# A fused attention and GEGLU kernel: batch 0's causal mask moved to TensorE, one normalisation per head pair, a third gate/value buffer, and batch 2's loads spread over batch 1

## The chip, the cores and the metric

The kernel runs on one core of a Trainium2 chip. The metric is the time of one execution on the device, in microseconds (us). A kernel is run several times, and the median is quoted with the lowest and highest run. The experiments were run in three sets, each on another chip (a1 to a4; b1 to b4; b5, c1, c2 and d1), with the kernel before beside each set: its medians were 399.49, 399.61 and 399.82 us. The ratios refer to these, and a difference between medians of two sets carries some tenths of a us for that.

One execution of each kernel was taken with the hardware profiler. Its span is about 1.7 us shorter than the device time of the same run (398.1 against 399.8 us before). The engines are PE (TensorE), DVE (VectorE), ACT (ScalarE), POOL (GpSimd) and SP (SyncE); PEld is TensorE's weight load. "The array" below is TensorE's.

## The reference

Eight batches of causal attention, with 16 "beacon" keys that every query may see. The result, regrouped as 4608 tokens of 512 numbers, goes through a GEGLU feed-forward.

```python
B, H, S, Nb, D = 8, 8, 576, 16, 64
k_all = concat([beacon_k, k], axis=2);  v_all = concat([beacon_v, v], axis=2)
scores = q @ k_all.T / sqrt(D)
scores = where(causal, -1e9, scores)       # causal only in the columns after the 16 beacons
a = softmax(scores);  attn = a @ v_all
x = attn.transpose(0, 2, 1, 3).reshape(4608, 512)
out = (gelu(x @ w_gate) * (x @ w_val)) @ w_out      # 512 -> 1536 -> 512
```

## The kernel before

The inputs are float32 and are converted as they are loaded; on the chip everything is bf16 with float32 accumulation in PSUM. Heads are handled in pairs, four pairs a batch. While batch b's attention runs, TensorE fills its waits with the output products (`out_mms`) of the chunk of tokens before; then comes batch b's feed-forward stage, the twelve gate/value products. Scores lie transposed (keys on partitions); each pair has four chunks of them, and each chunk gets one exponential on ScalarE and then its masks:

```python
def scores(b, m, c):
    ...
    for t, s_lo, w, col in CHUNKS[c]:
        for hi in range(2):
            r = slice(64 * hi, 64 * hi + 64)
            mm(s_ps[:, hi, col : col + w], qkT[r, m, 1, t * P : (t + 1) * P],
               qkT[r, m, 0, NB + s_lo : NB + s_lo + w], True, True)
    act(expT[:, :, o : o + w], s_ps[:, :, 0:w], ACT.Exp, scale=QK_SCALE)
    if b:
        masks(b, m, c)          # GpSimd: affine_select with 0.0, in place

# batch 0 only: masks(0, m, c, by_dve=True) takes the minimum with a 0 / 3e38 triangle on VectorE
```

The weighted sum of values carries the softmax denominator as a 65th column (`DV = 65`). Ten slots of 65 columns do not fit one bank, so they lie as six in one bank and four in the next, and the normalisation is done per bank:

```python
for c0, j0, n in ((0, 0, 6), (512, 6, 4)):
    x = x_ps[:, c0 : c0 + n * DV].rearrange("p (j d) -> p j d", d=DV)
    reciprocal(r, x[:, :, D:DV])
    tensor_tensor(out=y_sb[:, j0 : j0 + n, :], in0=x[:, :, 0:D], in1=r.to_broadcast([P, n, D]), op=mult)
```

`turn` then transposes `y_sb` on TensorE and `put` copies it to `xT_sb`, the input of the feed-forward. The order within a batch, and where loads are issued:

```python
if b:
    o(6); ab(0); o(8); cd(0); o(6); ab(1); o(4); av(b, 0); cd(1); o(4); turn(b, 0); put(b, 0)
    ...                                   # o(n): n output products; av: weighted sum + normalisation
    o(4); av(b, 3)
    gv_mms(b, 0, 0, 1, 2); turn(b, 3); put(b, 3); gv_mms(b, 1, 0, 1, 2); gv_mms(b, 0, 3); gv_mms(b, 1, 3)
for fi in range(F_TILES):                 # 12 gate/value products
    if fi < 2: gv_close(b, fi)            # GELU on ScalarE, product with the value half on VectorE
    else:      gate_val(b, fi)            # psum_s has two buffers of two banks
    ...
    if fi == 0:
        if b + 2 < B:
            load_qk(b + 2); load_v(b + 2)           # 17 loads, all issued by GpSimd
        if NPERM <= b + 1 < B:
            transpose_dma(b + 1)                    # keys and queries of batches 2 to 7, turned by DMA
```

GpSimd therefore has two jobs in one program order: it issues all the loads, and it masks the exponentials of batches 1 to 7.

The softmax here doesn't subtract the row's maximum and nothing guards it: scores larger than these inputs give would overflow.

## Time and profile before

| | before |
|---|---|
| device time, median of three (lowest to highest) | 399.53 us (399.45 to 400.36); 399.49 with the fourth run used below |
| span of the profiled run | 398.1 us, granted clock 0.987 |
| period of batches 2 to 6 (first output product of one attention stage to that of the next) | 42.60 us |
| period of batch 1 | 46.41 us (50.35 to 96.76) |
| from the first output product of batch 7 to the end | 88.35 us |

The page's first part for the kernel before, busy time, share of the span and number of instructions of each engine:

```profile
PE 377.9 (95%) x3014; PEld 183.4 (46%) x3014; DVE 166.9 (42%) x342; ACT 189.0 (47%) x254; POOL 159.8 (40%) x287
```

TensorE is the limit; a gain must come from the 5% in which it waits. The ends of matmuls in the trace are modelled, so gaps are read from starts: a 512-column matmul starts every 0.216 us, four of them take 0.87 us. The waits view of the kernel before, TensorE alone; the columns are what waits and for what, then us in all, times, and the longest:

```profile
PE gv_ps L161 <- DVE hT_sb L357: 6.9, 7, 1.0
PE x_ps L161 <- POOL expT L259: 1.6, 1, 1.6
```

The first wait comes seven times, once in each feed-forward stage after batch 0. The timeline shows one of them. A timeline line is: start, duration, engine, line, operation, output<-inputs, shape, count, and in brackets the idle time before it and what ended that (hT_sb, the "hidden product" below, is GELU of the gate half times the value half):

```profile
163.34 0.38 PE L161 MATMUL gv_ps<-xT_sb,wv_sb 128*128 128x512 bf16 x1
164.69 1.02 PE L161 MATMUL gv_ps<-xT_sb,wg_sb 128*128 128x512 bf16 x4 [0.98 <-DVE hT_sb L357]
```

The single value product would be followed 0.22 us after its start, at 163.56; the next one starts at 164.69. The time between, 1.13 us here (1.14 before rounding), is the wait for one of two gate/value buffers; 0.98 of it is in the brackets, the rest hidden by the modelled end of the matmul before. Seven such waits of 1.14 are 8.0 us.

Two further losses show little in the waits view. The first is in the turn of each pair; the timeline of TensorE in batch 3 of the kernel before:

```profile
146.37 1.08 PE L161 MATMUL x_ps<-v_sb,expT 128*128 128x65 bf16 x30
...
147.78 1.04 PE L161 MATMUL o_ps<-wo_sb,hT_sb 128*128 128x512 bf16 x4
148.88 0.45 PE L169 MATMUL y_ps<-ident,y_sb 128*128 128x128 bf16 x5
```

The four output products that cover VectorE's normalisation end at 147.78 + 0.87 = 148.65, but the turn starts at 148.88, 0.23 us later. VectorE's own timeline shows why, four chained operations from 147.49 to 148.83:

```profile
147.49 0.20 DVE L307 RECIPROCAL r_sb<-x_ps 128x6 f32<-128x6 f32 x1 [0.22 <-PE x_ps L161]
147.72 0.56 DVE L309 TENSOR_TENSOR y_sb<-x_ps,r_sb 128x384 bf16<-128x384 f32 x1
148.19 0.17 DVE L307 RECIPROCAL r_sb<-x_ps 128x4 f32<-128x4 f32 x1
148.40 0.43 DVE L309 TENSOR_TENSOR y_sb<-x_ps,r_sb 128x256 bf16<-128x256 f32 x1
```

The second is at the beginning of batch 1. Timeline of TensorE, kernel before:

```profile
56.43 1.04 PE L161 MATMUL o_ps<-wo_sb,hT_sb 128*128 128x512 bf16 x4
59.10 1.10 PE L161 MATMUL x_ps<-v_sb,expT 128*128 128x65 bf16 x15 [1.63 <-POOL expT L259]
60.43 1.01 PE L161 MATMUL x_ps<-v_sb,expT 128*128 128x65 bf16 x15 [0.24 <-DMA v_sb<-in_v_dram]
```

After 57.30 (56.43 + 0.87) the array has nothing until the first mask is done and it starts again at 59.10; a further wait of 0.24 us follows, and then 15 small matmuls take 1.01 us, twice the usual pace. The view puts the 0.24 us down to a transfer, but the fifth mask ends at 60.37 and the next matmul starts at 60.43, while batch 1's own values had landed by 49.61; so it is most likely the masks again. GpSimd's timeline of the same stretch shows what its masks waited behind: 6.07 us idle, ended by a transfer of the output weight, and then the issue of the loads themselves:

```profile
45.90 3.31 POOL L112 DMA_DIRECT2D q_sb<-in_q_dram  x4 [6.07 <-DMA wo_sb<-in_moe_w_out_dram]
...
54.37 4.27 POOL L112 DMA_DIRECT2D v_sb<-in_v_dram  x5
58.54 1.83 POOL L259 TENSOR_SCALAR_AFFINE_SELECT expT<-expT 128x224 bf16<-128x224 bf16 x5
```

The windows view of the kernel before, two stretches of 5 us (busy time with counts of PE, PEld, DVE, ACT, POOL; then PEclk, the granted TensorE clock; the recorded time of DMA packets over the time of the 16 DMA engines, which can exceed 1; GB/s):

```profile
10.00:15.00 5.00, 5.00 (x68) 2.92 (x65) 4.56 (x11) 3.66 (x5) 5.00 (x8) 0.50 2.17 162
...
60.00:65.00 5.00, 4.76 (x45) 2.42 (x42) 1.72 (x5) 1.89 (x3) 2.09 (x7) 0.66 0.79 95
```

In batch 0 (first line) ScalarE, VectorE, GpSimd and TensorE are all busy at a low recorded clock; the second line is the slow stretch after the wait in batch 1.

### The profile page before, as it was taken

Reading aid. Unit: us, or ns where it says so; the run is one execution under the profiler, and the core shown is the slowest. Engines: PE = TensorE matmul, PEld = TensorE weight load, DVE = VectorE, ACT = ScalarE, POOL = GpSimd, SP = SyncE. Lnnn points to the kernel's source line nnn. Section 1 sums busy time; section 2 is a strip of 40 time slices with the busy share of each in tenths; the row PEclk is TensorE's granted clock in tenths of the full one; section 3 lists DMA queues with packets and bytes.
Section 4 is the critical chain, followed back from the end, with each engine's and each line's share of the span. In section 5 each row is a group of like instructions: output and inputs, shape, how many; then the busy total and the mean of one; then the engine's idle time right before and its main releaser. Section 6 shows DMA issues by size and latency. Waiting matters only on the chain.

```text
span 398.1 us, 7407 instructions
## 1 busy us (share of the span) xinstructions
PE 377.9 (95%) x3014; PEld 183.4 (46%) x3014; DVE 166.9 (42%) x342; ACT 189.0 (47%) x254; POOL 159.8 (40%) x287
## 2 busy tenths in 40 slices
PE   6999989899999999899989999999989998999995
PEld 3464435444554445444544455444544454444442
DVE  2754634533363434432553344443534344333332
ACT  3763265424753387236733574348623772322210
POOL 8955394860468135841485047613300240000000
PEclk9799998999999999999999999999999999999999
DMA  7999994899139920997199915992141010000112
GB/s 106 178 206 204 177 159 59 96 145 109 54 65 146 143 57 29 134 148 75 55 96 141 92 54 83 140 127 63 45 102 28 30 54 26 2 0 28 43 50 91
DMA packets 140273, 36.24 MB, mean 91 GB/s; under 512 B 126928, under 2 KB 135632, under 8 KB 140240
## 3 DMA queue, kind: packets, MB, share of 16 engines
q0 software_dynamic: 104960, 19.13, 63.7%
q1 hardware_dynamic: 35280, 16.66, 21.5%
q8 instruction: 23, 0.38, 0.4%
q14 instruction: 10, 0.08, 0.1%
HBM read 38.27 MB, written 9.44 MB: 120 GB/s over the span
## 4 chain that ended last, share of the span: by engine, by line
PE 72%; DMA 11%; DVE 10%; POOL 3%; issue 1%; ACT 1%; POOLq 0%
PE gv_ps L161 39%; PE o_ps L161 19%; DVE y_sb L309 7%; PE x_ps L161 7%; DMA wo_sb<-in_moe_w_out_dram 5%; PE s_ps L161 4%; PE y_ps L169 3%; DMA wv_sb<-in_moe_w_val_dram 3%; DMA v_sb<-in_v_dram 3%; DVE r_sb L307 2%; DVE hT_sb L357 1%; POOL qk L112 1%; DMA k_sb<-in_k_dram 1%; ACT ge_sb L164 1%; POOL q_sb L112 1%
## 5 line engine op out<-in xcount | busy, mean ns | idle before, releaser
L164 ACT ACTIVATE ge_sb<-gv_ps 128x512 bf16<-128x512 f32 x108 | 63.6, 597 | 154.2 <-PE gv_ps L161 152.1
L357 DVE TENSOR_TENSOR hT_sb<-gv_ps,ge_sb 128x512 bf16<-128x512 f32 x108 | 74.0, 691 | 123.2 <-ACT ge_sb L164 123.2
L161 PE MATMUL gv_ps<-xT_sb,wg_sb 128*128 128x512 bf16 x432 | 113.8, 379 | 6.9 <-DVE hT_sb L357 6.9
L164 ACT ACTIVATE expT<-s_ps 128x1024 bf16<-128x1024 f32 (+3 forms) x128 | 103.6, 861 | 31.9 <-PE s_ps L161 31.5
L161 PE MATMUL gv_ps<-xT_sb,wv_sb 128*128 128x512 bf16 x432 | 113.8, 379 | 0.0
L161 PE MATMUL o_ps<-wo_sb,hT_sb 128*128 128x512 bf16 x432 | 108.0, 382 | 0.0
L259 POOL TENSOR_SCALAR_AFFINE_SELECT expT<-expT 128x256 bf16<-128x256 bf16 (+2 forms) x145 | 52.8, 388 | 131.8 <-ACT expT L164 131.8
L161 PEld LDWEIGHTS <-wg_sb 128*128 128x128 bf16 x432 | 41.0, 98 | 54.5 <-issue 8.8
L161 PEld LDWEIGHTS <-wv_sb 128*128 128x128 bf16 x432 | 42.2, 98 | 50.9
L161 PEld LDWEIGHTS <-hT_sb 128*128 128x128 bf16 x432 | 37.4, 98 | 49.8 <-issue 11.0
L385 DVE COPY o_sb<-o_ps 128x512 f32<-128x512 f32 x36 | 24.9, 690 | 44.9 <-PE o_ps L161 44.7
L112 POOL DMA_DIRECT2D v_sb<-in_v_dram x40 | 33.6, 855 | 15.0 <-DMA k_sb<-in_k_dram 5.7
L161 PEld LDWEIGHTS <-expT 128*128 128x128 bf16 (+1 forms) x960 | 33.6, 98 | 9.4 <-POOL expT L259 2.7
L161 PE MATMUL s_ps<-qkT 64*128 64x336 bf16 (+5 forms) x384 | 36.2, 290 | 1.2 <-ACT qkT L164 0.7
L161 PE MATMUL x_ps<-v_sb,expT 128*128 128x65 bf16 x930 | 34.3, 194 | 2.0 <-POOL expT L259 1.6
L309 DVE TENSOR_TENSOR y_sb<-x_ps,r_sb 128x384 bf16<-128x384 f32 (+1 forms) x62 | 30.4, 491 | 2.1
L112 POOL DMA_DIRECT2D q_sb<-in_q_dram x30 | 25.2, 859 | 6.1 <-DMA wo_sb<-in_moe_w_out_dram 6.1
L112 POOL DMA_DIRECT2D k_sb<-in_k_dram x30 | 25.5, 878 | 3.3 <-DMA q_sb<-in_q_dram 3.0
L307 DVE RECIPROCAL r_sb<-x_ps 128x6 f32<-128x6 f32 (+1 forms) x62 | 11.4, 184 | 35.7 <-PE x_ps L161 35.7
L161 PEld LDWEIGHTS <-qkT 64*128 64x128 bf16 x384 | 13.0, 96 | 17.2 <-issue 11.1
L328 DVE COPY xT_sb<-y_ps 128x576 bf16<-128x576 bf16 x31 | 14.1, 455 | 13.0 <-PE y_ps L169 13.0
L169 PEld LDWEIGHTS <-y_sb 128*128 128x128 bf16 (+1 forms) x160 | 9.3, 98 | 17.7 <-DVE y_sb L309 16.8
(41 smaller groups left out, 102.5 us busy)
## 6 DMA issues: line engine op xcount, KB each, us to landing
out_dram<-o_sb SPq DMA_DIRECT2D x36, 256.0 KB, 2.0
v_sb<-in_v_dram POOLq DMA_DIRECT2D x24, 128.0 KB, 9.8
q_sb<-in_q_dram POOLq DMA_DIRECT2D x24, 128.0 KB, 6.7
k_sb<-in_k_dram POOLq DMA_DIRECT2D x18, 128.0 KB, 9.8
wo_sb<-in_moe_w_out_dram POOLq DMA_DIRECT2D x1, 1536.0 KB, 18.4
wg_sb<-in_moe_w_gate_dram POOLq DMA_DIRECT2D x2, 512.0 KB, 11.2
wv_sb<-in_moe_w_val_dram POOLq DMA_DIRECT2D x2, 512.0 KB, 12.8
v_sb<-in_v_dram POOLq DMA_DIRECT2D x8, 112.0 KB, 9.0
```

The lines of the kernel that those rows point to most:

```text
L112: keep(nc.gpsimd.dma_start(out=out_ap, in_=in_ap))
L161: keep(nc.tensor.matmul(out_ap, lhsT, rhs, start=start, stop=stop, **kw))
L164: keep(nc.scalar.activation(out_ap, in_ap, func, **kw))
L169: keep(nc.tensor.transpose(out_ap, in_ap, ident[0:n, 0:n]))
L259: nc.gpsimd.affine_select(out=d, in_=d, pattern=[[0, 2], [1, n]], compare_op=ALU.is_ge, fill=0.0, base=NB if t == 0 else 0, channel_multip ...
L307: keep(nc.vector.reciprocal(r, x[:, :, D:DV]))
L309: nc.vector.tensor_tensor(out=y_sb[:, j0 : j0 + n, :], in0=x[:, :, 0:D], in1=r.to_broadcast([P, n, D]), op=ALU.mult)
L328: keep(nc.vector.tensor_copy(out_ap, y_ps[:, 0:S]))
L357: nc.vector.tensor_tensor(out=h_of[ci][:, fi, :], in0=gv_ps[:, 1, :], in1=ge_sb, op=ALU.mult)
L385: keep(nc.vector.tensor_copy(o_sb[:, ti, :], o_ps))
```

## The change

The intent, in five parts:

1. **Third gate/value buffer.** In batches 1 to 7 the third product takes the bank pair of `psum_x`, which is free by then. One gate/value half is moved ahead of the last turn.
2. **One normalisation per pair.** The two heads of a pair now lie in one bank each, five slots of 65 columns, so that one reciprocal and one product cover both banks.
3. **Batch 0's mask in PSUM.** Matmuls add -1e6 above the diagonal to the scores before the exponential; VectorE and GpSimd lose their mask steps there.
4. **Loads.** Batch 2's loads leave GpSimd's queue ahead of batch 1's masks. Its queries and keys are issued in and after batch 1's attention, its values after it. From batch 3 on, loads are issued two batches ahead as before.
5. **Order of batch 0**: transposes in halves, weighted sums in other banks, one pair's transposes of batch 1 moved into batch 1.

Part 3 rests on accumulation into part of a bank: the matmul of the scores starts the group, the mask matmuls that follow do not. The Trainium skill ("PSUM — Partial Sum Buffer", The four PSUM rules) says that a matmul without the first flag adds where a hidden written-bit is set and overwrites where it is not; this case agrees as far as its results go, for every run with these matmuls was correct against the reference.

```diff
 # scores(): batch 0's mask
+            diag = b == 0 and s_lo == S_LO[t]
             for hi in range(2):
                 mm(s_ps[:, hi, col : col + w], ...
-                    True, True,
+                    True, not diag, skip_group_check=True,
+            if diag:
+                base, n = (NB if t == 0 else 0), DIAG[t]
+                for k0, width in ((0, min(n, 64 - base)), (64, n)):
+                    for hi in range(2):
+                        r = slice(64 * hi, 64 * hi + 64)
+                        mm(s_ps[:, hi, col : col + width], eye[r, 64 - k0 : 192 - k0],
+                           neg[r, 64 - k0 + base : 64 - k0 + base + width], False, k0 == 64, ...)
 # normalize()
-        for c0, j0, n in ((0, 0, 6), (512, 6, 4)):
-            x = x_ps[:, c0 : c0 + n * DV].rearrange("p (j d) -> p j d", d=DV)
+        for x_ps, h0, h1 in x_of.pop(i):           # [(x, 0, 2)], a tile of two banks
+            x = x_ps[:, :, 0 : 5 * DV].rearrange("p b (j d) -> p b j d", d=DV)
             ... reciprocal, tensor_tensor
 # batch loop
+        loads = qk_loads(b + 1) if b == 1 else []  # 11 loads, handed out by ahead(n)
         ...
             cd(0)
+            ahead(2)                               # also after cd(1) and cd(2)
         ...
             gv_mms(b, 0, 0, 1, 2)
+            gv_mms(b, 1, 0)
             turn(b, 3)
             put(b, 3)
-            gv_mms(b, 1, 0, 1, 2)
+            gv_mms(b, 1, 1, 2)
         ...
-                gate_val(b, fi)
-            if b == 0 and fi >= 8:
-                transpose_pe(1, fi - 8)
+                if b and fi == 2:
+                    gv_mms(b, fi, *range(K_CHUNKS), pool=psum_x, tag="x")
+                    gv_close(b, fi)
+                else:
+                    gate_val(b, fi)
+            if b == 0 and 5 <= fi < 11:
+                transpose_half(1, (fi - 5) // 2, (fi - 4) % 2)
             if fi == 0:
-                if b + 2 < B:
+                ahead(len(loads))
+                if b == 1:
+                    load_v(b + 1)
+                if b and b + 2 < B:
                     load_qk(b + 2)
                     load_v(b + 2)
 # batch 0 (cut: its whole order was rewritten; mk() calls are gone)
     load_gate_val(4, 8)
+    load_qk6(1, 0, 4)
+    load_kb(1)
     load_gate_val(8, 12)
+    load_qk6(1, 4, H)
+    load_out_w()
+    load_v(1)
     ...
```

## The prediction

> **What bounds it now.** TensorE: the page shows it busy 377.9 of 398.1 us, granted clock 0.987. The gain must come from its waits. The timeline's matmul ends are modelled, so gaps are read from starts (a 512-column matmul starts every 0.216 us).
>
> Waits of TensorE before (timeline, chain, waits):
>
> 1. Start of each feed-forward stage, batches 1 to 7. The third gate/value product needs one of two buffers; its release (GELU 0.60 us, then product 0.70 us) ends 1.14 us after TensorE ran dry. The waits view lists 6.9 us; from starts it is 7 x 1.14 = 8.0 us.
> 2. Turning the attention output, four times a batch. VectorE runs reciprocal, product, reciprocal, product (1.37 us). TensorE arrives 0.23 us early for pairs 0 to 2 and 0.31 us for pair 3: 7 us in all.
> 3. Batch 1 attention: 27.7 us to its last early gate/value product, against 23.8 us in batches 2 and 3. GpSimd was held by transfers (6.07 us behind the output weight, then issues until 58.5 us), so its masks came late: a 1.63 us wait, 0.24 us more, then clock 0.66 for 5 us. The Trainium skill ("TensorE: Matmul & The Clock Gate", Part 1) says idle windows throttle the array; this trace agrees: 15 small matmuls took 1.10 us, twice the usual. Loss 3.9 us.
> 4. Batch 0: 29.2 us before the first uninterrupted feed-forward product. ScalarE's exponentials (13.0 us busy) run from 7.24 to 23.4 us with 3.2 us of holes; clock 0.71 from 10 to 20 us.
>
> **What the change does.**
> - Third buffer: removes item 1. Two products ahead of the last turn cover its 0.31 us.
> - One scaling over both banks: from the old pieces (384 columns 0.56, 256 columns 0.42 us) I estimate 0.84 us for 640; with one reciprocal of 0.21, latency 1.12 instead of 1.37 us. Covers the 0.23 us.
> - Batch 2 loads leave GpSimd's queue ahead of batch 1's masks: removes item 3.
> - Batch 0: VectorE loses its mask steps (about 3.5 us), GpSimd its masks; TensorE gains 80 small 64-row matmuls, estimated 0.6 us a pair from the score matmuls (8 in 0.4 us). I expect -1.7 us.
> - Cost: after batch 1's attention GpSimd issues 28 loads instead of 17 (about 2.9 instead of 1.8 MB, with 1.2 MB of transposes). At the 150 GB/s of the windows view GpSimd is free some 24.5 us later, about when batch 2's masks are due; batch 2's key transposes start some 4 us later. Expected wait 0.7 us, possibly 3.
>
> **On the critical path:** 8.0 + 6.3 + 3.8 + 1.7 - 0.7, about 19 us.
>
> **Predicted: 380.5 us; 8 in 10 within 377 to 386.** Faster by over 2%: 0.96; within 2%: 0.035; slower: 0.005.
>
> **What would show it.** Steady batch period 42.6 to about 40.5 us; no wait of gate/value products on the hidden product after batch 0; half as many scaling instructions, the product near 0.84 us; batch 1's masks following the exponentials at once, clock 1.0 there; batch 0's exponentials ending near 21.7, its feed-forward starting near 27.5 us.
>
> **What would make it wrong.** The two-bank product over 1.1 us; the buffer wait reappearing one product later; batch 2 waiting over 2 us for transposes or masks; batch 0 bound by TensorE at a low clock, the mask matmuls costing more than they free; transposes of later batches, landing some 2 us before their scores, becoming the limit.

## The result, and the profile after

The changed kernel took 383.89 us (382.35 to 385.59, four runs) against 399.49 us in the same rounds. The ratio is 0.9606 with a 95% interval of 0.9556 to 0.9655. Ratios here are those of the record, from fast runs of the same rounds, and are not quite the ratio of the medians quoted. The prediction of 380.5 us missed by 3.4 us; the time is inside the range. The outputs are right.

The page's first part for the kernel after; its profiled run took 384.87 us, with a span of 383.2 us:

```profile
PE 374.0 (98%) x3091; PEld 188.7 (49%) x3091; DVE 158.3 (41%) x272; ACT 189.6 (49%) x255; POOL 158.4 (41%) x283
```

TensorE's share rises from 95% to 98%. The trace has 77 more of its matmuls. Its waits, in the waits view of the kernel after; the wait for the hidden product is gone:

```profile
PE x_ps L174 <- POOL expT L282: 1.2, 1, 1.2
PE s_ps L174 <- ACT qkT L177: 0.7, 1, 0.7
PE s_ps L174 <- ACT expT L177: 0.7, 3, 0.3
```

The stage after the third buffer, in TensorE's timeline of the kernel after: the next product follows after 0.22 us, with no gap:

```profile
157.75 0.38 PE L174 MATMUL gv_ps<-xT_sb,wv_sb 128*128 128x512 bf16 x1
157.97 1.03 PE L174 MATMUL gv_ps<-xT_sb,wg_sb 128*128 128x512 bf16 x4
```

The turn, in the same timeline in batch 3, follows 0.87 us after the four output products and so at once:

```profile
141.76 1.08 PE L174 MATMUL x_ps<-v_sb,expT 128*128 128x65 bf16 x30
...
143.17 1.04 PE L174 MATMUL o_ps<-wo_sb,hT_sb 128*128 128x512 bf16 x4
144.04 0.44 PE L182 MATMUL y_ps<-ident,y_sb 128*128 128x128 bf16 x5
```

VectorE's timeline of the same pair has two operations in place of four, from 142.87 to 143.95, 1.08 us in place of 1.34:

```profile
142.87 0.22 DVE L332 RECIPROCAL r_sb<-x_ps 128x10 f32<-128x10 f32 x1 [0.22 <-PE x_ps L174]
143.13 0.82 DVE L334 TENSOR_TENSOR y_sb<-x_ps,r_sb 128x640 bf16<-128x640 f32 x1
```

In batch 1 the first weighted sum now follows 0.87 us after the start of the four output products before it (56.12), so the wait for masks there is gone:

```profile
56.99 1.08 PE L174 MATMUL x_ps<-v_sb,expT 128*128 128x65 bf16 x30
```

But the pattern that batch 1 had before is now in batch 2. TensorE's timeline of the kernel after:

```profile
96.60 1.04 PE L174 MATMUL o_ps<-wo_sb,hT_sb 128*128 128x512 bf16 x4
98.85 1.09 PE L174 MATMUL x_ps<-v_sb,expT 128*128 128x65 bf16 x15 [1.21 <-POOL expT L282]
100.17 1.00 PE L174 MATMUL x_ps<-v_sb,expT 128*128 128x65 bf16 x15 [0.24 <-DMA v_sb<-in_v_dram]
```

The output products end at 97.47, the first matmul after the masks starts at 98.85, the 0.24 us follow (the fifth mask ends at 100.12), and then 15 matmuls take 1.00 us as in batch 1 before. GpSimd's timeline of the kernel after shows the queue behind which these masks stood; the masks start at 98.36:

```profile
68.59 4.20 POOL L114 DMA_DIRECT2D k_sb<-in_k_dram  x5
...
77.44 3.57 POOL L114 DMA_DIRECT2D q_sb<-in_q_dram  x4
...
93.68 0.53 POOL L114 DMA_DIRECT2D v_sb<-in_beacon_v_dram  x1 [0.91 <-DMA q_sb<-in_q_dram]
94.20 4.19 POOL L114 DMA_DIRECT2D v_sb<-in_v_dram  x5
98.36 2.44 POOL L282 TENSOR_SCALAR_AFFINE_SELECT expT<-expT 128x224 bf16<-128x224 bf16 x7
```

Two stretches of the windows view of the kernel after, with the columns as before. In the first, batch 0, VectorE's busy time fell from 4.56 to 2.91 us; the second is the slow stretch after the wait, now in batch 2:

```profile
10.00:15.00 5.00, 4.86 (x82) 3.37 (x79) 2.91 (x6) 2.94 (x5) 5.00 (x7) 0.51 2.07 161
...
100.00:105.00 5.00, 4.83 (x39) 2.52 (x40) 1.50 (x3) 1.96 (x3) 1.83 (x6) 0.66 0.65 87
```

The stages, from the starts of each attention stage's first output product in the two traces:

| stage | before, us | after, us | difference |
|---|---|---|---|
| start to batch 1 | 50.35 | 49.31 | -1.04 |
| batch 1 | 46.41 | 41.16 | -5.25 |
| batch 2 | 42.60 | 44.28 | +1.68 |
| batches 3 to 6, each | 42.60 | 40.48 to 40.70 | -1.9 to -2.1 |
| batch 7 and the end | 88.35 | 86.26 | -2.09 |
| sum (span) | 398.1 | 383.2 | -14.9 |

Of the steady 2.12 us a batch (42.60 - 40.48), 1.14 is the buffer's wait, 3 x 0.23 = 0.69 the turns of pairs 0 to 2, and the remaining 0.29 the turn of pair 3, which the moved gate/value half covers. In the stages of batch 1 and of batch 2 the other differences have to be the loads and what depends on them: batch 1 gained 5.25 - 2.12 = 3.1 us, although it took over a pair's transposes, and batch 2 lost 1.68 + 2.12 = 3.8 us.

### The profile page after: what moved, and what is told of

It is laid out like the page before. It is cut to its first block, busy times and chain, and to the rows that moved or that the text cites. A ratio compares the mean times of both kernels' runs of the same rounds, so it can differ in the third digit from the quotient of the medians.

```text
span 383.2 us, 7484 instructions
## 1 busy us (share of the span) xinstructions
PE 374.0 (98%) x3091; PEld 188.7 (49%) x3091; DVE 158.3 (41%) x272; ACT 189.6 (49%) x255; POOL 158.4 (41%) x283
## 4 chain that ended last, share of the span: by engine, by line
PE 86%; DMA 6%; POOL 5%; ACT 1%; issue 1%; DVE 0%; POOLq 0%
PE gv_ps L174 43%; PE o_ps L174 24%; PE s_ps L174 8%; PE x_ps L174 7%; DMA q_sb<-in_q_dram 3%; PE y_ps L182 2%; POOL v_sb L114 2%; PE t_ps L182 1%; DMA qk<-in_q_dram 1%; ACT expT L177 1%; DMA v_sb<-in_v_dram 1%; POOL k_sb L114 1%; POOL qk L114 1%; POOL q_sb L114 1%; POOL expT L282 0%
## 5 line engine op out<-in xcount | busy, mean ns | idle before, releaser
L174 PE MATMUL gv_ps<-xT_sb,wg_sb 128*128 128x512 bf16 x432 | 115.0, 379 | 0.0
L282 POOL TENSOR_SCALAR_AFFINE_SELECT expT<-expT 128x256 bf16<-128x256 bf16 (+2 forms) x140 | 50.8, 386 | 122.7 <-ACT expT L177 122.7
L174 PE MATMUL s_ps<-qkT 64*128 64x336 bf16 (+5 forms) x384 | 37.1, 290 | 1.6 <-ACT qkT L177 0.7
L334 DVE TENSOR_TENSOR y_sb<-x_ps,r_sb 128x640 bf16<-128x640 f32 x31 | 25.6, 825 | 1.1
L174 PEld LDWEIGHTS <-qkT 64*128 64x128 bf16 x384 | 15.0, 95 | 17.8 <-issue 10.7
L332 DVE RECIPROCAL r_sb<-x_ps 128x10 f32<-128x10 f32 x31 | 6.8, 221 | 35.4 <-PE x_ps L174 35.4
L182 PEld LDWEIGHTS <-y_sb 128*128 128x128 bf16 (+1 forms) x160 | 10.3, 98 | 8.7 <-DVE y_sb L334 6.4
```

The lines of the kernel that those rows point to most:

```text
L174: keep(nc.tensor.matmul(out_ap, lhsT, rhs, start=start, stop=stop, **kw))
L182: keep(nc.tensor.transpose(out_ap, in_ap, ident[0:n, 0:n]))
L282: nc.gpsimd.affine_select(out=d, in_=d, pattern=[[0, 2], [1, n]], compare_op=ALU.is_ge, fill=0.0, base=NB if t == 0 else 0, channel_multip ...
L332: keep(nc.vector.reciprocal(r, x[:, :, :, D:DV]))
L334: nc.vector.tensor_tensor(out=y_sb[:, :, h0:h1, :].rearrange("p j b d -> p b j d"), in0=x[:, :, :, 0:D], in1=r.to_broadcast([P, h1 - h0, 5 ...
```

## The experiments

My theory was that the gain is the sum of its parts: third buffer about 8, normalisation and the fourth turn about 7, loads 3.8 in batch 1 less a loss in batch 2, batch 0 little. The first rival was that the change of loads moves batch 1's loss to batch 2 and gains next to nothing. The second was that the rest of the miss lies in batch 0, whose time the pace of the array decides. Twelve kernels were run. The expectations follow each edit; "the kernel after" is the base unless another is named.

To read them together, the same stage starts from each profile (one run each):

| kernel | first stage ends | batch 1 | batch 2 | batches 3 to 6 | run's time |
|---|---|---|---|---|---|
| before | 50.35 | 46.41 | 42.60 | 42.60 | 399.80 |
| d1, before with loads spread | 49.62 | 42.51 | 42.60 | 42.57 to 42.60 | 395.08 |
| after | 49.31 | 41.16 | 44.28 | 40.48 to 40.70 | 384.87 |
| a1, after again | 47.81 | 41.15 | 42.77 | 40.48 | 381.60 |
| a3, loads back | 48.56 | 48.61 | 40.49 | 40.48 | 387.57 |
| a4, no third buffer | 48.73 | 42.30 | 45.36 | 41.63 | 391.99 |
| b4, filler in batch 2 | 50.17 | 41.16 | 42.25 | 40.49 | 383.49 |
| a2, all loads spread | 48.29 | 41.16 | 40.48 | 40.49 | 379.85 |
| b1, a2 with two normalisations | 49.41 | 41.83 | 41.16 | 41.17 | 385.69 |
| b5, a2 without third buffer | 50.98 | 42.29 | 41.63 | 41.63 | 390.48 |
| b3, a2 with batch 0 reordered | 50.98 | 41.15 | 40.49 | 40.49 | 382.50 |
| b2, a2 with the old batch 0 | 50.87 | 40.42 | 40.49 | 40.48 | 381.70 |
| c1, a2 with the start filled | 48.55 | 41.15 | 40.49 | 40.49 | 380.08 |
| c2, c1 reordered | 48.17 | 41.15 | 40.49 | 40.49 | 379.68 |

The steady periods repeat to a few hundredths of a us from kernel to kernel and run to run. The first stage varies by 3 us. Periods are therefore the sharper instrument for the parts of the change that act in every batch.

### a1: the changed kernel again

No edit; more runs on another occasion.

> The changed kernel again, unedited, as the yardstick of this set: 382 to 386 us, ratio about 0.961. Its four earlier runs fell into two groups, 382.4 to 382.9 us (mean granted clock 1.0) and 384.9 to 385.6 us (0.982 to 0.987). If the groups are real, they show again with the same clocks, and the profile shows where the lower clock sits: theory, in batch 2 after its wait and in batch 0; rival, anywhere.

Measured: 384.61 us (381.60 to 386.84, six runs), ratio 0.9623 (0.9587 to 0.9658). The result repeats, and so does its spread of five us. The profile fell on the fastest run and differs from the first one in two places: the first stage is 1.5 us shorter, and in batch 2 the same wait (1.23 and 0.24 us) is followed by 15 matmuls in 0.63 us, not 1.00. So the wait is in the kernel, and the slow array after it comes in some executions only. In a1's run batch 2 lost 42.77 - 40.48 = 2.3 us, in the first 3.8. The two groups of runs with their own clocks, which the expectation asked for, did not come back: the slowest run (386.84) has a recorded clock of 0.996, a faster one (384.52) 0.987.

### a2: every batch's loads spread over the batch before

```diff
-        loads = qk_loads(b + 1) if b == 1 else []
+        loads = qk_loads(b + 1) if 1 <= b < B - 1 else []
 ...
-                if b == 1:
-                    load_v(b + 1)
-                if b and b + 2 < B:
-                    load_qk(b + 2)
-                    load_v(b + 2)
+                if 1 <= b < B - 1:
+                    load_v(b + 1)
```

No more than 17 loads are ever issued for a batch, and batch 3's are no longer in front of batch 2's masks.

> Each batch's loads are issued one batch ahead, as the change does for batch 2 alone, so GpSimd has 17 issues per batch instead of 28 after batch 1. Theory (batch 2's masks wait behind 28 issues on GpSimd; the wait of 1.2 + 0.24 us and the low clock after it cost 3.8 us): batch 2's period falls from 44.3 to 40.5 us, no wait for masks, total 380 to 381 us, ratio 0.951 to 0.954. Rival (the DMA engines are the limit, not the queue): the wait moves to another batch or to the scores that need the transposes, total 383 us or more.

Measured: 380.84 us (379.71 to 381.76), ratio 0.953 (0.9506 to 0.9555), whose interval does not touch that of the changed kernel in the same rounds. Batch 2 takes 40.48 us like every other. GpSimd's timeline in this kernel: the loads are done by 76.52, and after 16.14 us of idling the masks follow the exponential:

```profile
72.28 4.24 POOL L114 DMA_DIRECT2D v_sb<-in_v_dram  x5
92.65 0.38 POOL L282 TENSOR_SCALAR_AFFINE_SELECT expT<-expT 128x224 bf16<-128x224 bf16 x1 [16.14 <-ACT expT L177]
```

The loss in batch 2 is the queue of loads, and taking it away brings the kernel to the time that was predicted for the change (380.5).

### a3: the loads as they were before

```diff
-        loads = qk_loads(b + 1) if b == 1 else []
+        loads = []
 ...
-                if b == 1:
-                    load_v(b + 1)
-                if b and b + 2 < B:
+                if b + 2 < B:
```

> Batch 2's loads go back in front of batch 1's masks, all else as changed. Theory (the change only moved this loss from batch 1 to batch 2): batch 1's masks are late again by 1.5 to 2 us with a low clock after, batch 1 loses 3.5 to 4 us, batch 2 gains 3.8, total within 1 us of the changed kernel: 383 to 385 us, ratio 0.958 to 0.964. Rival (the move itself gained 3.8 us as predicted and batch 2's loss has another cause): 386.5 to 388 us.

Measured: 385.67 us (384.21 to 387.57), ratio 0.9651 (0.9628 to 0.9675). Batch 2 has no loss (40.49), batch 1 has it: 48.61 us, 7.5 more than in the changed kernel. The median lies between the range of the theory (383 to 385) and that of the rival (386.5 to 388), so the total decides for neither. TensorE's timeline of this kernel in batch 1; the first number in brackets is the idle time:

```profile
60.73 2.36 PE L174 MATMUL x_ps<-v_sb,expT 128*128 128x65 bf16 x30 [4.33 <-POOL expT L282]
```

The wait was 4.33 us, where I had written 1.5 to 2, and the 30 small matmuls after it took 2.36 us against 1.08 in a fast array. I had taken the wait over from the kernel before; but the array's work now ends at 56.23 in place of 57.30, as batch 1 starts earlier, while GpSimd's masks start at 60.30 in place of 58.54: it waits longer for the output weight (6.72 in place of 6.07 us, to 47.51 in place of 45.90). On this profile, its slowest run, the change's new order of loads gained 7.5 us in batch 1 and lost 2.3 to 3.8 in batch 2. The totals show much less: 1.1 us between the medians of a3 and a1, and their intervals overlap. What can be said is that the loss went from one batch to the next, and that the net gain of this part is not resolved by the totals. a2 shows what it could have been: 4.8 us between its median and a3's.

### a4: no third buffer

```diff
-                if b and fi == 2:
+                if False:
```

> The third gate/value product of batches 1 to 7 goes back to the pair of buffers; the two products moved ahead of the last turn stay. Theory: TensorE stalls again 1.1 us at each of 7 feed-forward starts, +7.7 to 8.0 us: 391 to 393 us, ratio 0.979 to 0.984, and the waits view lists some 6.9 us on the hidden product. Rival (the moved products give the release more time, so the buffer is worth only part): +4 us or less.

Measured: 390.48 us (389.67 to 391.99), ratio 0.9784 (0.9759 to 0.9809; unclear at 2%). The period is 41.63, 1.15 us longer in every batch, which is 8.0 us in seven, and the waits view lists the 6.9 us on the hidden product again; the medians differ from a1's by 5.9, less than I had put down. Both have batch 2's wait and a wide spread (a1's runs span 5.2 us), so I asked the question again on a2, as b5.

### b5: no third buffer, on a2

The edit is the same, on a2.

```diff
-                if b and fi == 2:
+                if False:
```

> On the version with all loads one batch ahead, the third gate/value product back in the pair of buffers. The same edit on the changed kernel cost 5.9 us where 7.7 to 8.0 were expected, with a disturbed batch 2 on both sides. Theory (7 waits of 1.14 us, and the missing part was noise of batches 0 and 2): steady period 41.6 us, total 388 to 389.5 us, ratio 0.971 to 0.975. Rival (part of the buffer's gain is lost elsewhere): 386.5 to 387.5 us.

Measured: 390.01 us (389.52 to 390.48), ratio 0.9757 (0.9736 to 0.9777), 9.2 us over a2's median and above the range expected. The period is 41.63 again, so 8.0 us by the periods. The other 1.2 or so is consistent with a slower first stage in these runs (50.98 us in the profile, the slow case of b3 below), which is not shown for the runs that were not profiled. The third buffer is worth its 8.0 us.

### b1: two normalisations again, on a2

```diff
-            x_of[i] = [(x, 0, 2)]
+            x_of[i] = [(x[:, 0:1, :], 0, 1), (x[:, 1:2, :], 1, 2)]
```

> On the version with all loads one batch ahead (380.84 us, ratio 0.953), the scaling of a pair goes back to two reciprocals and two products, one per bank; layouts stay. Theory (TensorE waits for the chain of four at three turns a batch; the fourth is covered by the moved products): +0.2 to 0.25 us a turn, 21 turns, +4.2 to 5.3 us: 385 to 386 us, ratio 0.963 to 0.967, steady period 41.1 to 41.2 us instead of 40.48. Rival (the turns were paced by something else, and the period fell for the third buffer alone): no change.

Measured: 386.43 us (385.65 to 387.52), ratio 0.9678 (0.965 to 0.9706). The period is 41.17, 0.69 more than a2's, so 4.8 us in seven batches, and 5.6 by the medians. That is three turns of 0.23 us in each batch; pair 3's turn stays covered by the moved gate/value half. The Trainium skill ("VectorE: DVE Perf Modes", the rules for kernel authors) says of chained VectorE operations that one should minimise their count; this trace agrees, the same 640 columns take 1.34 us in four operations and 1.08 in two.

### b2: batch 0 as before, on a2

The edit puts back the kernel before's triangle, VectorE and GpSimd masks and its whole order of batch 0 (`diag = False`, `mk(...)`, `transpose_pe`), and leaves everything else of a2.

```diff
-            diag = b == 0 and s_lo == S_LO[t]
+            diag = False
 ...
-    transpose_half(0, 1, 1)
-    c(0, 1)
-    ...
+    transpose_pe(0, 1)
+    mk(0, AB)
+    c(0, *CD)
+    ...                       # the order of the kernel before, to the last line of batch 0
-            if b == 0 and 5 <= fi < 11:
-                transpose_half(1, (fi - 5) // 2, (fi - 4) % 2)
+            if b == 0 and fi >= 8:
+                transpose_pe(1, fi - 8)
```

> On the same version, batch 0 as before the change: masks by VectorE and GpSimd on the exponentials, the old order of work, batch 1's transposes in the old places. Theory (what the two profiles at the same low clock show: feed-forward of batch 0 starts only 0.4 us earlier; up to 1.9 us where the clock is full): +0.4 to 1.9 us, 381.3 to 382.8 us, ratio 0.954 to 0.958. Rival (the prediction's -1.7 us holds on average and more): 382.5 us or above.

Measured: 381.56 us (381.37 to 381.75, four runs), ratio 0.9549 (0.9525 to 0.9573), 0.7 us over a2's median (of another set); the intervals overlap, so this is not resolved. The part of the change with the most code is worth 0.7 us by the medians and perhaps nothing, where I had predicted 1.7.

### b3: another order of transposes and scores in batch 0, on a2

```diff
     transpose_half(0, 2, 1)
-    transpose_half(0, 2, 0)
     c(1, *AB)
+    transpose_half(0, 2, 0)
     transpose_half(0, 3, 1)
     c(1, 1)
```

ScalarE had a hole of 1.7 us before its fifth exponential in the changed kernel; this order gives it work earlier.

> On the same version, pair 1's first two score chunks of batch 0 stand in front of pair 2's q transposes, which wait for a load. Theory (ScalarE's hole of 0.6 to 1.7 us after its fourth exponential is this order): the hole shrinks to under 0.4 us and the total falls 0.3 to 0.8 us: 380 to 380.5 us, ratio 0.951 to 0.952. Rival (the batch is bound by the later loads or the clock): within 0.2 us, the hole comes back at pair 2 or 3.

Measured: 381.21 us (379.26 to 382.50), ratio 0.9535 (0.9504 to 0.9566): no gain over a2 that can be seen, but its runs fall in three pairs, near 379.3, 381.2 and 382.5. The profile fell on a 382.5. TensorE's timeline of that run, early in batch 0:

```profile
8.25 0.69 PE L182 MATMUL t_ps<-ident,qk 96*64 96x96 bf16 x12
```

Twelve transposes took 0.69 us. In runs with a short first stage the same groups take 0.45, as in c1 below. The windows view of the same run puts the clock at full from 5 us on; in the second of its stretches two more such groups started and took 0.69 us:

```profile
5.00:10.00 5.00, 4.25 (x70) 3.05 (x70) 1.66 (x4) 2.61 (x4) 5.00 (x9) 1.00 1.13 139
10.00:15.00 5.00, 5.00 (x86) 3.56 (x84) 3.03 (x6) 3.29 (x5) 5.00 (x7) 1.00 2.11 156
```

So the recorded clock (1.00) does not agree with the pace of the array. The Trainium skill ("TensorE: Matmul & The Clock Gate", Part 1, the caveats on HAM traces) says that the clock events of a trace are unreliable; this run agrees. The groups of transposes served as my clock from here on. In the profiles, batch 0's feed-forward starts (first uninterrupted product) at 27.3 to 28.2 us in a1, a2, a3, a4, c1 and c2, whose groups are mostly fast, at 30.48 us in b3 and b5, whose groups are all slow, and between in the rest (28.82 in the kernel after, 28.92 in b1, 29.68 in b4). The old batch 0 starts it at 28.49 us in d1, and at 29.22 and 29.73 us in the kernel before and b2, the last all slow. The new order is thus about as good as its luck: its start moves by 3.2 us with the pace (27.32 to 30.48), and with all groups slow it is 0.75 us behind the old (30.48 - 29.73). No profile of the old order has a mostly fast array, so its lead there is not measured; it is 1.9 us only against a mostly slow one (29.22 - 27.32). In the profiles of the new order without filler the pace also goes with the set: mostly fast in a1 to a4, slow for half or more of the groups in b1, b3, b4 and b5.

### b4: filler in front of batch 2's wait, on the changed kernel

```diff
             o(4)
+            if b == 2:
+                warm(7, psum_x, "x")      # seven matmuls whose results are not used
             av(b, 0)
```

This leaves the wait for the masks in place but keeps the array working through it.

> The changed kernel with seven idle matmuls of 512 columns (1.5 us at full clock) put in front of batch 2's first attention product, where TensorE waits for masks. They fill the wait and cannot shorten it. Theory (part of the 3.8 us is the clock that falls after the wait): the clock in the 5 us after stays 1.0 and the 15 following matmuls keep 31 ns spacing, batch 2's period 42.5 to 43 us in every run, total 383 to 383.5 us, with the runs above 384 us gone. Rival (the low clock does not cost anything beyond the wait): unchanged, or 0.3 us slower.

Measured: 383.49 us (383.14 to 385.03), ratio 0.9606 (0.9581 to 0.9631). TensorE's timeline in batch 2 of this kernel:

```profile
98.34 1.67 PE L174 MATMUL w_ps<-idle 128*128 128x512 bf16 x7
100.07 1.11 PE L174 MATMUL x_ps<-v_sb,expT 128*128 128x65 bf16 x30
```

The small matmuls after the wait start at a normal pace, 30 in 1.11 us, at a granted clock of 1.0, and batch 2 took 42.25 us, 2.0 less than in the first profile. But the total did not move by an amount that the runs resolve, and runs above 384 us did not vanish (384.21, 385.03). So the slow array after batch 2's wait is real where it occurs and is not the whole of the spread; the rest may sit in the first stage, which took 50.17 us in this profile. The Trainium skill (same page, Part 1 and the table of advice) says that an idle window of about 3.4 us halves the clock, and advises against TensorE gaps over about 3 us. Single idle times of 1.63 (before), 1.21 (after) and 1.12 us (a4), each with another 0.24 behind it, were followed by a recorded clock of 0.66 and a slow array (in a4 about 3 us later, where five transposes took 0.73 us and not 0.44). Counted from the end of the output products to the matmul behind the fifth mask, these are stretches of 3.1, 2.7 and 2.6 us with only 15 small matmuls in them, which is not far from the page's figure. In a1 such a stretch of 2.7 us was not followed by a slow array; in a3 a wait of 4.33 us without a break was.

### c1: the start filled, on a2

```diff
     transpose_half(0, 0, 0, by_act=True)
+    warm(3, psum_x, "x")
     c(0, *AB)
```

Before the first scores TensorE waits for ScalarE's copy (0.7 us in the waits view above). Three matmuls fill that wait.

> On the version with all loads one batch ahead (380.84 us, 379.7 to 381.8), three idle matmuls fill TensorE's 0.75 us wait before the first scores. Theory (batch 0 is a lottery: in eight profiles of the new batch 0 its feed-forward starts between 27.3 us, where all groups of twelve transposes take 0.45 us, and 30.5 us, where all take 0.69 us; the early wait decides when the array turns fast): the groups from 7.5 us on take 0.45 us, feed-forward from 27.3 to 28.3 us, all runs between 379.3 and 380.5 us. Rival (the turn is decided by something that this wait does not touch): runs as before, 379.5 to 382 us, or 0.3 to 0.5 us slower for the filler.

Measured: 379.94 us (379.61 to 380.08, five runs), ratio 0.9503 (0.9484 to 0.9522). Against a2 the median falls by 0.9 us, within overlapping intervals; what changed is the spread, 0.5 us where a2 has 2.1. a2 ran on another chip, so the control is b5, which ran beside c1 without the filler: its groups were all slow, and its four runs less the 8.0 us of the buffer come to 381.5 to 382.5 us. TensorE's timeline of this kernel, the same place as in b3:

```profile
8.01 0.45 PE L182 MATMUL t_ps<-ident,qk 96*64 96x96 bf16 x12
```

From 8.01 us on every group of twelve takes 0.45 us. In the five runs timed, and in the four of c2, no run fell behind. A narrow spread alone proves little, for b2, with the old batch 0, all groups slow and no filler, had 0.4 us over its four runs.

### c2: c1 with b3's order

```diff
     transpose_half(0, 0, 0, by_act=True)
+    warm(3, psum_x, "x")
     ...
     transpose_half(0, 2, 1)
-    transpose_half(0, 2, 0)
     c(1, *AB)
+    transpose_half(0, 2, 0)
```

> The same with pair 1's first score chunks in front of pair 2's q transposes, the edit that was unclear because its profile fell in the slow array. Theory: with a fast array the hole of ScalarE before its fifth exponential shrinks from 1.0 to under 0.4 us, 379 to 380 us, 0.3 us under the run without the reorder. Rival: no difference.

Measured: 379.57 us (379.36 to 380.04), ratio 0.9497 (0.9478 to 0.9516), the best median of all, 4.3 us under the change itself. ScalarE's hole before the fifth exponential shrinks from 0.78 to 0.21 us and the feed-forward starts at 27.68 in place of 28.06 us; the totals of c1 and c2 overlap, so the reorder alone is not shown to gain.

### d1: the kernel before with only the loads spread

This is the kernel before with `qk_loads` and `ahead` as in a2, and nothing else of the change.

```diff
+        loads = qk_loads(b + 1) if 1 <= b < B - 1 else []
 ...                            # ahead(2) after cd(0), cd(1) and cd(2)
             if fi == 0:
-                if b + 2 < B:
-                    load_qk(b + 2)
-                    load_v(b + 2)
+                ahead(len(loads))
+                if 1 <= b < B - 1:
+                    load_v(b + 1)
```

> The kernel before with one thing changed: each batch's loads one batch ahead, from batch 1 on. Theory (late masks cost 3.9 us in batch 1 and nothing need be paid for it later): no wait for masks in batch 1 or 2, batch 1's stage falls from 27.7 to 23.8 us, total 395.3 to 396 us, ratio 0.989 to 0.992. Rival (removing the wait only uncovers another in batch 1): 397 us or above.

Measured: 395.99 us (395.08 to 396.34), ratio 0.9902 (0.9883 to 0.9921). Batch 2 is unharmed (42.60), batch 1's loss is gone, and the gain is 3.8 us between the medians. This is what my prediction took for its item 3, 3.8 us, but only with the loads of every batch a batch ahead.

## Why the prediction was right or wrong

**Right**: faster by 3.9%, inside 377 to 386 us. The limit was read rightly too: TensorE's waits were the place to gain, and each of the repeated waits vanished where it was expected to.

**Third buffer: right.** 8.0 us were predicted; the period shows 1.15 us a batch (a4, b5), 8.0 in seven. The wait did not reappear one product later.

**Normalisation and fourth turn: right.** 6.3 us were predicted. The product took 0.82 us where 0.84 was estimated, the chain 1.08 where 1.12 was. b1's period gives 4.8 us for the normalisation. The fourth turn, 0.29 us in each of seven batches and so about 2.0, is worked out from the two periods and was not undone by itself.

**Loads: right in mechanism, mis-sized in the term "Expected wait 0.7 us, possibly 3".** The prediction counted the queue after batch 1, 28 loads in place of 17, and put GpSimd's release 24.5 us later. In the trace the last wait of the queue ends at 93.68, 25.1 us after its start at 68.59. What was left out is the issue of the loads that are still to come after that: 0.53 us for the beacon rows and 4.19 for five more loads of v, so the masks begin at 98.36, 29.8 us after the start. Of these 29.8 us 7.1 are GpSimd's waits for earlier transfers (the sum of the brackets in its whole timeline) and the rest is the issue of the 28 loads, which an estimate from the bandwidth leaves out; that its 24.5 us came near the 25.1 is therefore partly luck. The 4.7 us (98.36 - 93.68) are more than the 1.38 us of array wait, since TensorE still had output products to do until 97.47. The second part left out is what follows the wait: the 0.24 us, and in some executions a slow array. The loss was 2.3 us (a1) to 3.8 (the first profile). The Trainium skill ("DMA: Bandwidth & Descriptors", the anatomy of one DMA on the gpsimd path) calls descriptor generation "small, variable"; here one load that writes 128 KB in rows of 128 bytes (converted from float32) held GpSimd for 0.84 us (4.19 / 5), and in an engine that also masks this is on the critical path.

**Batch 0: right in direction, mis-sized in the term "I expect -1.7 us".** The profiled first stage was 1.04 us shorter, and 0.74 of this is the pair's transposes that went into batch 1; the feed-forward started at 28.82 in place of 29.22 us, 0.4 earlier, where "near 27.5" was predicted. The exponentials ended at 22.96 where 21.7 was. The risk was named in the list ("bound by TensorE at a low clock") but not given a size. The pace of the array decides: 27.3 us in a1 at a fast array, 30.5 in b3 and b5 at a slow one. a1's 27.32, with exponentials ending at 21.26, is what was predicted, so the prediction's figures are those of a fast array, set against a profile of the kernel before that was mostly slow; hitting them in a given run is luck.

**The sum.** 19 us were predicted from a base of 399.5; 15.6 came. Of the 3.4 us missing, 1.6 to 3.1 is batch 2's loss (2.3 to 3.8 against 0.7) and 1.3 batch 0's (0.4 against 1.7). The fourth turn and the transposes moved to batch 1 pull in opposite directions by less than a us each. a2, with batch 2's loss taken away, comes to 380.84 and c1, with the start settled as well, to 379.94. That is the support for the split; a2 and b4 show the first term, while the second rests on b2 and the profiles and stays unresolved in the totals.

**What stays open.** Why the array starts fast in one execution and slow in the next is not known; c1 and c2 show only that with the wait before the first scores filled nine runs agreed, on one chip and in one set. The net worth of the change's own order of loads (a1 against a3) is within the spread.

## What to carry to other kernels

If an engine both issues loads and computes, count the loads' issue time in its queue as work in front of its next computation, up to the last load; a burst of loads that is moved from one stage to the next moves the wait with it, while a steady lead of one stage removes it (a2 and d1); batches 3 to 6 of the kernel after, with a steady lead of two, have none either. Measure edits that act in every stage by the stage's period, which repeated here to hundredths of a us, where totals spread over several. A short wait of TensorE can cost twice, as the wait and again in a slower array; filling waits of about a us with matmuls whose results are thrown away is a cheap thing to try, and near the start the filled runs here (c1, c2) were steady.

## What the Trainium skill lacked or had wrong

- "TensorE: Matmul & The Clock Gate" (Part 1 and the advice table) warns of TensorE gaps over about 3 us. It gives no figure for gaps with a little work in them. Here waits of 1.1 to 1.6 us that belong to stretches of 2.6 to 3.1 us with only 15 small matmuls were followed by a slow array in three profiles (before, after, a4; in the kernel after 15 small matmuls took 1.00 us in place of 0.63), and not in a fourth, a1, with a stretch of 2.7 us.
- The same page, Part 4, says that the full clock does not engage for transpose mode. Here groups of twelve 96x64 transposes took 0.69 us in a slow array and 0.45 in a fast one, so transposes do profit from a fast array; whether transposes alone would bring it about is not shown.
- The same page's caveat on unreliable clock records held: 1.00 was recorded for 10 to 15 us of b3, while groups of transposes took the slow 0.69 us. The page names a metric of throttled time as a cross-check; the time of a repeated group of equal instructions served here.
- That the slow start of the array differs from run to run is in the same page (Part 1), so it is not lacking. Its size here: the first stage ended between 47.81 and 50.98 us with the new batch 0. The page has no case of a short wait at the start that is filled; here the runs with 0.7 us of wait filled spread by 0.5 us (c1), and a2's, on another chip, by 2.1.
- "DMA: Bandwidth & Descriptors" (anatomy of the gpsimd path) gives descriptor generation as "small, variable" with no number. Here it held GpSimd 0.84 us for a load that writes 128 KB in 128-byte rows and 0.53 us for one that writes 16 KB.
